# Small tiles of 32 bytes between the weight slots of an attention and feed-forward kernel

## The chip, the cores and the metric

One core of a Trainium2 chip. The metric is the device time of one execution in microseconds; lower is better. The kernel before takes 937.57 us (median of 3 runs, 937.54 to 937.85).

## The reference

Linear attention with random features, then two feed-forward layers, in float32:

```
attention, for each head:  phi(x) = exp(h - max h) / sqrt(m),  h = x omega' - |x|^2 / 2
    kv = phi(k)' v;  z = sum of phi(k);  out = phi(q) kv / (phi(q) z + 1e-6)
x = attention, 2304 tokens x 512
layer 1:  h = x @ w_in;   g = max(0.01 h, h);            x = g @ w_out      (w_in 512 x 2048, w_out 2048 x 512)
layer 2:  h = x @ w_in2;  g = h * clip(h + 3, 0, 6) / 6;  x = g @ w_out2
```

## The kernel before

The 2304 tokens go in five groups of 512, 256, 512, 512 and 512. Layer 1 takes a group at a time, and the attention of the next group lies between its matmuls; then layer 2 goes over the groups again. Every large product is made of float32 values that are split into a high and a low half of type fp32r, three matmuls for one (`mm3`, L440): high weights by high data (L441), low by high (L442), high by low (L443).

The lines name a matmul as `bank<-moving,stationary`: the operand that streams through and the weights that are loaded ahead of it. The weight loads are rows of PEld. So `bank<-x,w` is a matmul whose weights lie in a `w` slot while an `x` tile streams. The stationary operand is 128 x 128; the columns of a matmul are those of the moving one, 512 or 256.

A layer works on the 2048 hidden columns in 16 blocks of 128. In layer 1 the H part of a block moves the four `x` tiles (the split input) against a slot of `w_in`, 12 matmuls, and the O part moves the block's `g` against a slot of `w_out` into four accumulators, 12 matmuls. In layer 2 the four groups of 512 tokens take blocks in pairs (`Hpair`): the H product of two blocks is made of seven products of 256 columns (L811), whose weights are sums and differences of weight blocks, held in `w` slots (`c`), and whose moving operands are the input tiles or sums of them (`x` slots, or `w` slots). The O part moves `w_out` (512 columns of a slot) against `g` or a second `g` that lies in a `w` slot. The group of 256 tokens goes block by block with 256 columns.

All these operands live in slots, fixed tiles of SBUF that are handed out by a planner (`Graph.run`): it puts the operations of all engines in one order, by estimated costs and due times, and each operation is then emitted in that order. Its costs are of an operation's size and engine; an address is in none of them. The slots, by where they lie:
- In the pool `const`, in this order: 18 slots `w0` to `w17`, four `x`, three `g` (each two tiles of [128, 512], the halves, 2048 bytes a partition and tile), then `ident`, `wn`, `three` and `zero` (512, 512, 64 and 768 bytes).
- Behind `const`, in pools that are opened when earlier ones close: `first` (staging and attention tiles), then `second` (11 slots more of the kind `w`, L396) and `stage`, then `third` (3 more, L404). They are named `second_w` and `third_w` in the profile. Slots with an index of 24 or more are preferred for the operands of L811.
- In the pool `misc`, at the other end: staging for weights (`wst`, `wt`) and input (`xr`), scratch `u`, and small tiles: six `nm` and three pairs `den` ([128, 4, 1], 16 bytes of data in 32), three `sq`.

A tile of an operand is 2048 bytes, a multiple of 256. So all `w`, `x` and `g` tiles lie at one residue modulo 256 bytes, and `second_w` and `third_w`, behind 1856 bytes of further tiles, 64 bytes above it.

`nm` holds the negated maxima of the features (written by VectorE and POOL, read by ACT as a bias), `den` the denominators of the attention.

Of the kernel before, what the change touches and what calls it, by code (L numbers as in the profile page):

```python
# [9 lines left out]
F32R = mybir.dt.float32r  # L10
# [15 lines left out]
FT = DFF // 128  # L26
# [5 lines left out]
NLATE = 14  # L32
# [284 lines left out]
def attn_moe_kernel(ctx: ExitStack, tc: tile.TileContext, qT, kT, qn, kn, v1, om2, w1i, w1o, w2i, w2o, out):  # L317
# [6 lines left out]
    g = Graph()  # L324
# [6 lines left out]
    misc = ctx.enter_context(tc.tile_pool(name="misc", bufs=1, side="right"))  # L331
# [3 lines left out]
    def sb(name, shape, dt=F32, pool=const):  # L335
        return pool.tile(shape, dt, name=name)

    def many(n, name, *specs, pool=const):
        return [tuple(sb(f"{name}{i}_{j}", *s, pool=pool) for j, s in enumerate(specs)) for i in range(n)]

    x1 = [[dram.tile([128, 2, GN[i]], F32, name=f"x1_{i}_{k}") for k in range(KT // 2)] for i in range(NG)]

    stage = [("wst", ([128, 512, 2], U32)), ("wt", ([128, 512], U32))]
    slots = {
        "w": many(2 * FT - NLATE, "w", ([128, 512], F32R), ([128, 512], F32R)),
        "x": many(KT, "x", ([128, 512], F32R), ([128, 512], F32R)),
        "g": many(3, "g", ([128, 512], F32R), ([128, 512], F32R)),
        "wst": many(2, *stage[0], pool=misc),
        "wt": many(2, *stage[1], pool=misc),
        "xr": many(KT, "xr", ([128, 512],), pool=misc),  # L350
        "u": many(2, "u", ([128, 512],), pool=misc),
        "nm": many(6, "nm", ([128, 4, 1],), pool=misc),
        "den": many(3, "den", ([128, 4, 1],), ([128, 4, 1],), pool=misc),
        "sq": many(3, "sq", ([128, 9, 1],), pool=misc),
        "junk": many(1, "junk", ([128, 4, 128], BF16), pool=misc),
        "raw": [],
    }


    late = {  # L360
# [607 lines left out]
    for at, grp in enumerate(ORDER2):  # L968
        n = GN[grp]
# [99 lines left out]
```

## Time and profile before

| | |
|---|---|
| device time, median of 3 runs | 937.57 us |
| span of the profiled execution | 935.4 us |
| TensorE matmul busy | 926.9 us (99%) |
| TensorE weight load busy (beside matmuls) | 785.2 us (84%) |
| VectorE busy | 595.2 us (64%) |
| ScalarE busy | 521.0 us (56%) |
| GpSimd busy | 239.6 us (26%) |
| share of TensorE in the chain that ended last | 95% |
| granted TensorE clock, all 40 slices | 0.9 or more |

A matmul's duration in the profile is longer than the distance to the next matmul's start, since matmuls overlap; the busy time is the union. A mean of a group mixes the first matmul of a block, which may wait for its operand, with the others.

### The profile page before, as it was taken

What the parts mean: (1) busy time and instruction counts of PE and PEld (TensorE: products, weight loads), DVE (VectorE), ACT (ScalarE), POOL (GpSimd) and SP (SyncE); (2) the same over time, 40 slices, a digit from 0 to 9 for tenths busy, and PEclk for the clock granted to TensorE, in tenths of its full rate; (3) what the DMA queues carried; (4) which work ended last, traced back from release to release, by engine and by line L of the source; (5) the groups of instructions that cost most, each with busy time, mean ns of one, the idle gap of its engine ahead of it and who ended that gap; (6) DMA issues with size and microseconds to landing.
All of it is one profiled execution on the core that took longest, in us unless ns stands there. A gap on an engine that the chain in (4) does not pass through costs nothing.

```text
span 935.4 us, 15350 instructions
## 1 busy us (share of the span) xinstructions
PE 926.9 (99%) x5678; PEld 785.2 (84%) x5678; DVE 595.2 (64%) x1373; ACT 521.0 (56%) x1207; POOL 239.6 (26%) x349
## 2 busy tenths in 40 slices
PE   8999999999999999999999999999999999999998
PEld 8878777899778787777788898888888888888887
DVE  6898978734732223233587799888669657865642
ACT  7867767754643344333433576567566556655543
POOL 3445444312410012111000023343334234330000
PEclk9999999999999999999999999999999999999999
DMA  9457645333211211000454341101002000200010
GB/s 330 137 163 233 186 141 157 110 90 87 63 40 40 67 45 57 12 0 1 158 158 135 113 159 55 59 22 69 1 1 69 23 1 1 68 1 1 2 46 22
DMA packets 40186, 73.04 MB, mean 78 GB/s; under 512 B 10032, under 2 KB 19376, under 8 KB 40112
## 3 DMA queue, kind: packets, MB, share of 16 engines
q1 hardware_dynamic: 40112, 72.07, 24.2%
q8 instruction: 44, 0.72, 0.3%
q14 instruction: 30, 0.25, 0.1%
HBM read 62.62 MB, written 9.44 MB: 77 GB/s over the span
## 4 chain that ended last, share of the span: by engine, by line
PE 95%; DVE 2%; ACT 1%; DMA 0%; issue 0%; SPq 0%; POOL 0%
PE bank L441 23%; PE bank L442 22%; PE bank L443 22%; PE bank L811 16%; PE bank L563 4%; PE bank L609 3%; PE bank L739 2%; PE bank L716 1%; PE bank L620 1%; PE bank L650 1%; ACT first_h L543 1%; DMA first_xn<-kn 0%; DVE second_w L430 0%; PE bank L584 0%; DVE wst L474 0%
## 5 line engine op out<-in xcount | busy, mean ns | idle before, releaser
L874 DVE TENSOR_TENSOR g<-bank,g 128x512 fp32r<-128x512 f32 (+1 forms) x96 | 57.6, 600 | 120.8 <-ACT g L427 120.5
L872 ACT ACTIVATE bank<-bank 128x512 f32<-128x512 f32 (+1 forms) x80 | 43.8, 547 | 103.8 <-PE bank L443 103.6
L532 DVE TENSOR_REDUCE nm<-bank 128x4 f32<-128x512 f32 (+3 forms) x92 | 49.5, 568 | 53.5 <-PE bank L563 53.0
L427 ACT COPY late_u<-bank 128x256 f32<-128x256 f32 (+1 forms) x103 | 38.9, 380 | 79.3 <-PE bank L811 75.3
L543 ACT ACTIVATE h<-bank,nm 128x128 f32<-128x128 f32 x208 | 58.6, 391 | 29.6 <-POOL nm L538 29.3
L538 POOL TENSOR_TENSOR nm<-nm,sq 128x4 f32<-128x4 f32 (+3 forms) x92 | 21.9, 251 | 196.3 <-DVE nm L535 194.3
L441 PE MATMUL bank<-x,w 128*128 128x512 f32 (+1 forms) x188 | 70.8, 377 | 0.0
L441 PE MATMUL bank<-g,w 128*128 128x512 f32 (+1 forms) x180 | 69.2, 384 | 0.0
L443 PE MATMUL bank<-x,w 128*128 128x512 f32 (+1 forms) x188 | 68.7, 366 | 0.0
L442 PE MATMUL bank<-x,w 128*128 128x512 f32 (+1 forms) x188 | 68.6, 365 | 0.0
L443 PE MATMUL bank<-g,w 128*128 128x512 f32 (+1 forms) x180 | 66.4, 369 | 0.0
L442 PE MATMUL bank<-g,w 128*128 128x512 f32 (+1 forms) x180 | 66.3, 368 | 0.0
L441 PE MATMUL bank<-x,second_w 128*128 128x512 f32 (+1 forms) x160 | 57.2, 357 | 0.0
L442 PE MATMUL bank<-x,second_w 128*128 128x512 f32 (+1 forms) x160 | 55.8, 349 | 0.0
L443 PE MATMUL bank<-x,second_w 128*128 128x512 f32 (+1 forms) x160 | 55.8, 349 | 0.0
L442 PE MATMUL bank<-w,g 128*128 128x512 f32 x138 | 54.5, 395 | 0.0
L427 ACT CAST g<-bank 128x512 fp32r<-128x512 f32 (+1 forms) x95 | 49.5, 521 | 8.8 <-DVE bank L869 6.5
L441 PE MATMUL bank<-w,g 128*128 128x512 f32 x138 | 54.3, 394 | 0.0
L443 PE MATMUL bank<-w,g 128*128 128x512 f32 x138 | 53.8, 390 | 0.0
L811 PEld LDWEIGHTS bank<-x,second_w 128*128 128x128 f32 x330 | 42.2, 188 | 3.6 <-ACT late_u L427 2.0
L811 PE MATMUL bank<-x,second_w 128*128 128x256 f32 x330 | 44.8, 281 | 0.0
L441 PEld LDWEIGHTS bank<-x,w 128*128 128x128 f32 x188 | 35.4, 188 | 9.8 <-issue 3.0
(274 smaller groups left out, 2597.0 us busy)
## 6 DMA issues: line engine op xcount, KB each, us to landing
wst<-w2i SPq DMA_DIRECT2D x16, 512.0 KB, 3.5
wst<-w2o SPq DMA_DIRECT2D x16, 512.0 KB, 3.6
v<-v SPq DMA_DIRECT2D x14, 330.0 KB, 3.0
wst<-w1i SPq DMA_DIRECT2D x9, 512.0 KB, 4.3
wst<-w1o SPq DMA_DIRECT2D x9, 512.0 KB, 4.2
xr<-x SPq DMA_DIRECT2D x16, 256.0 KB, 3.3
xn<-kn SPq DMA_DIRECT2D x14, 256.0 KB, 2.9
xT<-kT SPq DMA_DIRECT2D x13, 256.0 KB, 2.7
```

The costliest lines, as they stand in the source:

```text
L427: return [("act", c_act(n, psum), lambda: nc.scalar.copy(dst(), src())), dve if psum else dve + (True,)]
L441: nc.tensor.matmul(o, lhsT=ah, rhs=bh, start=start, stop=False)
L442: nc.tensor.matmul(o, lhsT=al, rhs=bh, start=False, stop=False)
L443: nc.tensor.matmul(o, lhsT=ah, rhs=bl, start=False, stop=stop)
L532: g.op([("dve", c_dve(c * 128), lambda raw=raw, n_=n_: nc.vector.tensor_reduce(out=n_()[:, :, 0], in_=raw(), axis=AX.X, op=ALU.min))], rd= ...
L538: ("pool", 170, lambda n_=n_, s_=s_: nc.gpsimd.tensor_tensor(out=n_(), in0=n_(), in1=s_(), op=ALU.subtract))],
L543: nc.scalar.activation(h.tiles[0][:, q * 128:q * 128 + 128], raw()[:, q], AF.Exp, bias=nm.tiles[0][:, q], scale=-1.0)
L563: nc.tensor.matmul(ps[bank].tiles[0][o, i * 128:i * 128 + 128], lhsT=src.tiles[0][r, i * 128:i * 128 + n], rhs=wn[r], start=True, stop=True)
L609: nc.tensor.matmul(p.tiles[0][:, w], lhsT=l, rhs=r, start=n == 0, stop=n == len(todo) - 1, skip_group_check=True)
L811: nc.tensor.matmul(R[r](), lhsT=w[x], rhs=m[y], start=start and k == i == 0, stop=k == 1 and i == 2, skip_group_check=True)
L872: g.op([("act", c_act(n, True), lambda: nc.scalar.activation(P(), P(), AF.Prelu, alpha=0.01))], wr=[p], due=d)
L874: g.op([("dve", c_dve(n), lambda: nc.vector.tensor_tensor(out=G1(), in0=P(), in1=G0().bitcast(F32), op=ALU.subtract))], rd=[p, (gg, 0)], w ...
```

## The change

Ten of the small tiles (six `nm`, four `den`) move from `misc` to `const`: one behind every second `w` slot up to the sixteenth, one behind `g0` and one behind `g1`. The last pair of `den` stays in `misc`, behind `sq`, which moves ahead of `wst`. Each takes 32 bytes a partition. The number of slots of each kind stays, and so does the sum of bytes in use. By the sizes, relative to `x`: `w0`, `w1` at residue 0, `w2`, `w3` at 32, and so on to `w14`, `w15` at 224 and `w16`, `w17` at 0; `g0`, `g1`, `g2` at 0, 32 and 64; `second_w` and `third_w` at 128.

```diff
--- before.py
+++ after.py
@@ -341,20 +341,37 @@
     x1 = [[dram.tile([128, 2, GN[i]], F32, name=f"x1_{i}_{k}") for k in range(KT // 2)] for i in range(NG)]
 
     stage = [("wst", ([128, 512, 2], U32)), ("wt", ([128, 512], U32))]
+    small = {"nm": [], "den": []}
+    shifts = ["nm"] * 6 + ["den"] * 5
+
+    def shift():
+        t = shifts.pop(0)
+        small[t].append(sb(f"{t}{len(small[t])}", [128, 4, 1]))
+
+    def spread(n, name, every):
+        out = []
+        for i in range(n):
+            out.append(tuple(sb(f"{name}{i}_{j}", [128, 512], F32R) for j in range(2)))
+            if i % every == every - 1 and i < n - 1:
+                shift()
+        return out
+
     slots = {
-        "w": many(2 * FT - NLATE, "w", ([128, 512], F32R), ([128, 512], F32R)),
+        "w": spread(2 * FT - NLATE, "w", 2),
         "x": many(KT, "x", ([128, 512], F32R), ([128, 512], F32R)),
-        "g": many(3, "g", ([128, 512], F32R), ([128, 512], F32R)),
+        "g": spread(3, "g", 1),
+        "sq": many(3, "sq", ([128, 9, 1],), pool=misc),
         "wst": many(2, *stage[0], pool=misc),
         "wt": many(2, *stage[1], pool=misc),
         "xr": many(KT, "xr", ([128, 512],), pool=misc),
         "u": many(2, "u", ([128, 512],), pool=misc),
-        "nm": many(6, "nm", ([128, 4, 1],), pool=misc),
-        "den": many(3, "den", ([128, 4, 1],), ([128, 4, 1],), pool=misc),
-        "sq": many(3, "sq", ([128, 9, 1],), pool=misc),
         "junk": many(1, "junk", ([128, 4, 128], BF16), pool=misc),
         "raw": [],
     }
+    while len(small["den"]) < 6:
+        small["den"].append(sb(f"den{len(small['den'])}", [128, 4, 1], pool=misc))
+    slots["nm"] = [(x,) for x in small["nm"]]
+    slots["den"] = list(zip(small["den"][::2], small["den"][1::2]))
 
 
     late = {
```

## Rows read from the trace of the kernel before

**Rows 1.** The page, parts 1 and 4: busy us (share, instructions); share of the chain.

```profile
PE 926.9 (99%) x5678; PEld 785.2 (84%) x5678; DVE 595.2 (64%) x1373; ACT 521.0 (56%) x1207; POOL 239.6 (26%) x349
...
PE 95%; DVE 2%; ACT 1%; DMA 0%; issue 0%; SPq 0%; POOL 0%
```

**Rows 2.** Waits of the weight loads: us in total, times, longest.

```profile
PEld bank L811 <- ACT late_u L427: 6.1, 30, 0.3
```

**Rows 3.** L441 from 461 to 504: ns min/median/max, first and last start.

```profile
L441 PE MATMUL bank<-x,w x35: 389/389/389, 460.8 to 503.0; 128*128 128x512 f32 x35
L441 PE MATMUL bank<-g,w x29: 389/389/389, 465.6 to 503.7; 128*128 128x512 f32 x29
```

**Rows 4.** The same line from 511 to 545, two groups of four.

```profile
L441 PE MATMUL bank<-x,second_w x20: 393/396/398, 511.9 to 536.4; 128*128 128x512 f32 x20
...
L441 PE MATMUL bank<-g,third_w x4: 393/396/398, 542.7 to 544.8; 128*128 128x512 f32 x4
```

**Rows 5.** Stretches: length, PE, PEld, DVE, ACT, POOL busy us, clock, DMA share, GB/s.

```profile
460.00:500.00 40.00, 40.00 (x178) 33.12 (x177) 29.31 (x52) 16.56 (x28) 2.19 (x2) 1.00 0.45 143
511.00:545.00 34.00, 34.00 (x147) 27.42 (x146) 28.14 (x51) 16.28 (x31) 2.93 (x2) 1.00 0.29 91
```

**Rows 6.** Groups by form, layer 1, 512 columns: busy us, mean ns | idle before.

```profile
L442 PE MATMUL bank<-x,w 128*128 128x512 f32 x144 | 56.2, 390 | 0.0
...
L442 PE MATMUL bank<-x,second_w 128*128 128x512 f32 x96 | 37.9, 395 | 0.0
...
L442 PE MATMUL bank<-g,second_w 128*128 128x512 f32 x80 | 31.6, 396 | 0.0
...
L442 PE MATMUL bank<-g,third_w 128*128 128x512 f32 x32 | 12.7, 396 | 0.0
```

**Rows 7.** Groups by form, layer 2, 512 columns.

```profile
L442 PE MATMUL bank<-w,g 128*128 128x512 f32 x138 | 54.5, 395 | 0.0
...
L443 PE MATMUL bank<-w,g 128*128 128x512 f32 x138 | 53.8, 390 | 0.0
...
L442 PE MATMUL bank<-w,w 128*128 128x512 f32 x56 | 21.9, 391 | 0.0
...
L442 PE MATMUL bank<-w,second_w 128*128 128x512 f32 x40 | 15.8, 395 | 0.0
...
L443 PE MATMUL bank<-second_w,w 128*128 128x512 f32 x20 | 7.9, 394 | 0.0
L442 PE MATMUL bank<-second_w,w 128*128 128x512 f32 x20 | 7.8, 391 | 0.0
```

**Rows 8.** L442 from 217.4 to 221, 256 columns: ns min/median/max.

```profile
L442 PE MATMUL bank<-x,second_w x7: 276/276/279, 217.6 to 221.0; 128*128 128x256 f32 x7
```

**Rows 9.** Groups by form, 256 columns.

```profile
L811 PE MATMUL bank<-x,second_w 128*128 128x256 f32 x330 | 44.8, 281 | 0.0
...
L811 PE MATMUL bank<-x,third_w 128*128 128x256 f32 x258 | 34.9, 281 | 0.0
L811 PE MATMUL bank<-second_w,second_w 128*128 128x256 f32 x234 | 32.8, 282 | 0.0
...
L811 PE MATMUL bank<-x,w 128*128 128x256 f32 x180 | 25.9, 284 | 0.0
...
L442 PE MATMUL bank<-x,second_w 128*128 128x256 f32 x64 | 17.9, 279 | 0.0
...
L811 PE MATMUL bank<-second_w,w 128*128 128x256 f32 x54 | 7.5, 280 | 0.0
```

**Rows 10.** ACT's groups by line: busy us, mean ns | idle before, releaser.

```profile
L427 ACT CAST second_w<-wst 128x512 fp32r<-128x512 f32 x33 | 20.5, 622 | 3.8 <-DVE wst L434 3.1 <-PE bank L811 0.3
...
L427 ACT CAST w<-wt 128x512 fp32r<-128x512 f32 x16 | 10.0, 624 | 13.7 <-DVE wt L483 13.7
```

**Rows 11.** Timeline of TensorE, second and eighth matmul after a break: start us, us.

```profile
86.64 0.39 PE L442 MATMUL bank<-g,w 128*128 128x512 f32 x1
...
88.03 0.39 PE L442 MATMUL bank<-g,w 128*128 128x512 f32 x1
```

## The prediction

> **What bounds the kernel now.** I read the page's busy table and the chain first: TensorE is busy 926.9 of 935.4 us and holds 95% of the chain [rows 1]. So a step of another engine counts only where TensorE waits for it, and its largest wait of that kind, 6.1 us in 30 pieces, is for values copied out of PSUM [rows 2]. The span is 2.2 us below the 937.57 us median; I take that remainder as constant and add changes to the median.
>
> What is left is how long TensorE needs for one matmul. Two views say that this is not one number. From 460.8 to 503.7 us every first matmul of a triple takes 389 ns [rows 3]: 64 of them, 63 steps of three matmuls in 42.9 us, 227.0 ns apart. From 511.9 to 544.8 us the same shape takes 393 to 398 ns [rows 4] (two of four such groups stand there): 48 of them, 47 steps, 32.9 us / 141 = 233.3 ns apart. So duration and spacing differ alike (6.5 and 6.3 ns), and durations stand for spacings below. Both stretches have full clock and a TensorE that never pauses; VectorE is busy 73% in one and 83% in the other, DMA 45% and 29% [rows 5], no likely cause of 6.5 ns on every matmul. What differs without exception is the stationary operand, `w` slots in one, `second_w` and `third_w` in the other. By the sizes of their tiles `w`, `x` and `g` lie at one residue modulo 256 and the later slots 64 bytes above it. The groups of all lines agree [rows 6]: 390 against 395 or 396.
>
> So I read a price per pair of residues: (residue of the weights) minus (residue of the moving tile). At 512 columns: offset 0 costs 1 ns above 389 on average, +64 costs 6.5 [rows 6], −64 (`second_w` moving against `w`) 2 to 5 [rows 7]. At 256 columns it is the other way round: the shortest row is 276 ns at +64 [rows 8], in most of layer 2 the same offset shows 281, offset 0 shows 282 to 284, −64 shows 280 [rows 9].
>
> **The change part by part.** Order, waits, DMAs and counts stay as they are: the planner's costs hold no address. ACT's casts take 622 ns into `second_w` and 624 into `w` [rows 10], two residues 64 apart, so I cost the new residues at nothing for ACT, and likewise for VectorE and POOL, which write the low halves and the small tiles that move; the cover, if that is wrong, is that TensorE waits little for any of them [rows 2]; without it, 2 ns on the some 1200 instructions of ACT [rows 1] would be 2.4 us. What remains is TensorE's price list. After the change the 18 `w` slots lie at eight residues (four of them at that of `x`, two at each other), `g` at 0, +32 and +64, and `second_w` and `third_w` at +128 from `x`, because ten small tiles push the pools behind them by 320 bytes. Five of the eight offsets (32, 96, 128, 160, 224) occur nowhere in the trace. The nearest rows are +1 and +6.5 at 512 columns, with −64 at 2, 2 and 5 in between; I take 2.5 for an offset that is not 0 or +64, with 1 and 6.5 as ends. At 256 columns the ends are 0 and 8 and the nearest rows (−64, 280; +64, 281) give 4; for +128 I take 3.5, for the rest 4.
>
> Layer 1, 512 columns, weights in `w`: 144 a line with `x` moving and as many with `g`, on three lines, 864 matmuls [rows 6], now +1. After: 4/18 at 1, 2/18 at 6.5, 12/18 at 2.5, mean 2.6. That is +1.4 us (ends +0.5 and +3.7).
> Layer 1, weights in later slots: 3 x (96 + 16 + 80 + 32) = 672 [rows 6] (the 16 are `x` against `third_w`, like the 32 with `g`), now +6.5. Moving `x` (336) goes to 128, 2.5: −1.3. Moving `g` (336) goes to 128, 96 and 64, mean (2.5 + 2.5 + 6.5) / 3 = 3.8: −0.9. Sum −2.2 (ends −3.1 and 0).
> Layer 2, 512 columns, `w` or `second_w` moving: 828 matmuls, among them `w` against `g` 414 at about +4, `w` against `second_w` 120 at +6, `w` against `w` 168 at +2.3 [rows 7], 3.3 us of excess in all. After: spread over eight offsets, (1 + 6.5 + 6 x 2.5) / 8 = 2.8 each, 2.3 us: −1.0 (ends −1.9 and +1.5).
> 256 columns, `x` against later slots: 828 matmuls, 330 + 258 in L811 and 48 at +5, 192 at +3 [rows 9]: 3.8 us. After, at 3.5: 2.9, so −0.9 (ends −3.8 and +2.9). `x` against `w`, 180 in L811 [rows 9] and 132 in L441 to L443, at +7.5: spread 4/18 at 7.5, 14/18 at about 4, mean 4.8: −0.8 (ends −1.7 and 0). `g` against `w`, 108, in the same ratio: −0.2. The 414 products with both operands in later slots, 234 of them `second_w` with itself [rows 9], keep their offset 0, since both move together: 0, and 0 for the 162 mixed ones, which have no common direction.
> Settling: in a run at offset 0 that follows a break, the six steps from its second matmul on take 1.39 us, 231.7 ns each where 227.0 is the settled value [rows 11], 28 ns for six. Today neighbouring blocks of 12 matmuls have one offset; with alternating slot residues each of 128 layer-1 blocks may settle anew, at most 3.6 us. Part of it is already in the mean prices, so +1.5 (ends 0 and 3.6).
>
> Sum: 1.4 − 2.2 − 1.0 − 0.9 − 0.8 − 0.2 + 1.5 = −2.2 us, 935.4 us; I give **935.5 us**, the rounding of the terms being of that size. All ends together would be 927 and 949.
>
> The rule that speaks against any effect: the Trainium skill, "TensorE: Matmul & The Clock Gate", section "Step-by-step: what each phase is for", says that the running matmul and the loading of the next weights read SBUF through two separate ports, so that one takes nothing from the other; "SBUF — State Buffer", section "Who interferes with whom", says that TensorE never waits on anyone. By these the sum would be zero. The rows do not bear that out: one shape, one clock, 227.0 and 233.3 ns [rows 3, 4].
>
> **The rivals.**
> F, faster: only the offsets +64 at 512 columns and 0 at 256 are bad, and every other one is about as good as the best. With 1.5 for the untried ones at 512 columns and 3 at 256, the parts are +0.8, −2.8, −1.6, −2.5 and 0.5 for settling: −5.6, **932.0 us**. For it: at 256 columns the best offset is +64, so 0 is nothing special. Against: −64 already costs 2 to 5 at 512.
> S, slower: the low price at offset 0 is a lock that any other offset loses. Place: the 864 layer-1 matmuls on `w`, of which 14/18 leave offset 0. With 5.5 for the untried ones at 512 and 5 at 256 the parts are +3.1, −0.6, +0.9, −0.2 and +1.5: +4.7, **942.3 us**. The point from which it decides: with p the price of the untried offsets at 512, the three 512-column terms sum to 1.76 p − 6.2 us; with −1.8 and +1.5 added, the total passes +1.9 us at p = 4.8 and falls below −1.9 at p = 2.6. For it: 64 of 64 durations at 389 look like a lock, and +64 loses it fully. Against: −64 loses only a third to a half of it.
> N, nothing: the difference belongs to the slot itself or to its time in the kernel, not to the residues. Then **937.6 us**. For it: `second_w` and `third_w` are used late, with other neighbours on the engines. Against: within layer 2 `w` and `second_w` alternate and keep their own prices [rows 7].
> A part of N can also hold: the change gives `second_w` and `third_w` one residue, not eight, so more than half of the 256-column matmuls see one new offset or none.
>
> **How the numbers follow.** About 0.2% (1.9 us) is what a measurement tells from no change, so "same" is 935.7 to 939.4. The forecast (p between 1.8 and 4.8, own range 934 to 939) has 0.47: it lies across the border, 0.20 of it faster, 0.27 same. F has 0.20, all faster. S has 0.23, all slower. N has 0.07, same. The rest, 0.03, is half faster, half slower. Faster 0.42, same 0.34, slower 0.24. The range reaches into F and S until about 0.1 is left beyond each end: 931.0 to 942.2.
>
> **What would show it.** In the changed kernel's groups by form, `x` against `w` at 512 columns no longer has one duration of 389 ns over a whole stretch but steps from block to block with the slot (389 at four slots of 18); its mean of 390 rises to some 391 or 392 (S: 394 and more; F: under 390.5; N: unchanged). `x` against `second_w` at 512 columns falls from 395 to about 391.5 (S: 394; F: 390). In L811 `x` against `second_w` goes from 281 to between 276 and 284, and `second_w` against `second_w` stays at 282. Neither VectorE's nor ACT's durations move, and the waits [rows 2] stay within a microsecond. The forecast is wrong if 389 and 396 appear as before with the same slots, if the +128 price at 256 columns is at 0 or 8 (3 us either way), or if TensorE's idle time grows, which nothing in this sum holds.

## The result and the profile after

The changed kernel takes 943.7 us (942.79 to 943.8), 1.0061 times the kernel before (interval 1.0042 to 1.0081): 6.1 us slower. The span of the profiled execution is 942.0 us, where 935.4 us stood before. Line numbers are 17 higher than before: L458 to L460 are the three lines of `mm3`, L828 is L811.

The page of the changed kernel, parts 1 and 4:

```profile
PE 933.9 (99%) x5678; PEld 788.0 (84%) x5678; DVE 594.8 (63%) x1373; ACT 521.5 (55%) x1207; POOL 240.4 (26%) x349
...
PE 95%; DVE 2%; ACT 1%; DMA 0%; issue 0%; SPq 0%; POOL 0%
```

TensorE's busy time grew by 7.0 us, from [rows 1], with the same 5,678 matmuls; VectorE, ScalarE and GpSimd stand within a microsecond, and the chain has the same shares. So TensorE doesn't wait more for the other engines: the matmuls themselves became slower.

The groups of the changed kernel by form (busy us, mean ns | idle before), first 512 columns, then 256:

```profile
L459 PE MATMUL bank<-g,w 128*128 128x512 f32 x144 | 56.6, 393 | 0.0
L459 PE MATMUL bank<-x,w 128*128 128x512 f32 x144 | 56.7, 394 | 0.0
L459 PE MATMUL bank<-x,second_w 128*128 128x512 f32 x96 | 37.8, 394 | 0.0
L459 PE MATMUL bank<-g,second_w 128*128 128x512 f32 x80 | 31.6, 395 | 0.0
...
L459 PE MATMUL bank<-w,g 128*128 128x512 f32 x138 | 54.5, 395 | 0.0
L460 PE MATMUL bank<-w,g 128*128 128x512 f32 x138 | 54.5, 395 | 0.0
L459 PE MATMUL bank<-w,w 128*128 128x512 f32 x56 | 22.1, 394 | 0.0
...
L828 PE MATMUL bank<-x,second_w 128*128 128x256 f32 x330 | 45.5, 283 | 0.0
L828 PE MATMUL bank<-x,w 128*128 128x256 f32 x180 | 25.8, 283 | 0.0
L828 PE MATMUL bank<-second_w,second_w 128*128 128x256 f32 x234 | 32.7, 282 | 0.0
```

`x` against `w`, 390 ns in [rows 6], takes 394, and `g` against `w` takes 393; its row in the kernel before:

```profile
L442 PE MATMUL bank<-g,w 128*128 128x512 f32 x144 | 56.1, 390 | 0.0
```

The later slots, which were to gain from offset 128, stay at 394 and 395. In layer 2 `w` against `g` has lost the 390 of one of its lines [rows 7] and `w` against `w` goes from 391 to 394. At 256 columns `x` against `second_w` rises from 281 to 283 [rows 9], and `second_w` against itself, whose two operands move together, keeps 282.

The first line of a triple between 461 and 504 us, the stretch of [rows 3], as min/median/max:

```profile
L458 PE MATMUL bank<-x,w x32: 389/394/404, 462.8 to 501.2; 128*128 128x512 f32 x32
L458 PE MATMUL bank<-g,w x28: 391/396/401, 468.3 to 504.0; 128*128 128x512 f32 x28
```

Before, each of these was 389. In this stretch `x` meets eight slots, one at each residue, and `g` none at its own. The `x` blocks at the offsets 0 and 32, four matmuls of this line each:

```profile
L458 PE MATMUL bank<-x,w x4: 389/389/393, 462.8 to 464.8; 128*128 128x512 f32 x4
L458 PE MATMUL bank<-x,w x4: 392/395/396, 465.5 to 467.6; 128*128 128x512 f32 x4
```

Only the block at the residue of `x` keeps 389. The step from block to block with the slot, which the prediction named as its sign, is there; its height is that of rival S.

The remaining steps of the prediction: the waits of the weight loads (us in total, times, longest), then ACT's casts into `w` (busy us, mean ns | idle before), then the first stretch of [rows 5] with the same columns:

```profile
PEld bank L828 <- ACT late_u L444: 5.8, 28, 0.3
```

```profile
L444 ACT CAST w<-wt 128x512 fp32r<-128x512 f32 x16 | 10.0, 623 | 13.1 <-DVE wt L500 13.1
```

```profile
460.00:500.00 40.00, 40.00 (x174) 32.31 (x173) 26.65 (x47) 16.88 (x28) 1.29 (x1) 1.00 0.45 144
```

Against [rows 2] and [rows 10] next to nothing moved: 5.8 for 6.1 us, 623 for 624 ns. The clock is 1.00 again and TensorE never stops, but 40 us hold 174 matmuls where they held 178.

### The profile page after: what moved, and what is told of

The parts are those of the page before. It is cut to its first block, busy times and chain, and to the rows that moved or that the text cites. A ratio compares the mean times of both kernels' runs of the same rounds, so it can differ in the third digit from the quotient of the medians.

```text
span 942.0 us, 15350 instructions
## 1 busy us (share of the span) xinstructions
PE 933.9 (99%) x5678; PEld 788.0 (84%) x5678; DVE 594.8 (63%) x1373; ACT 521.5 (55%) x1207; POOL 240.4 (26%) x349
## 4 chain that ended last, share of the span: by engine, by line
PE 95%; DVE 2%; ACT 1%; DMA 0%; issue 0%; SPq 0%; POOL 0%
PE bank L458 23%; PE bank L460 22%; PE bank L459 22%; PE bank L828 16%; PE bank L580 4%; PE bank L626 3%; PE bank L756 2%; PE bank L733 1%; PE bank L637 1%; PE bank L667 1%; ACT first_h L560 1%; DMA xn<-qn 0%; DVE second_w L447 0%; PE bank L601 0%; DVE wst L491 0%
## 5 line engine op out<-in xcount | busy, mean ns | idle before, releaser
L458 PE MATMUL bank<-x,w 128*128 128x512 f32 (+1 forms) x188 | 71.2, 379 | 0.0
L458 PE MATMUL bank<-g,w 128*128 128x512 f32 (+1 forms) x180 | 69.7, 387 | 0.0
L460 PE MATMUL bank<-x,w 128*128 128x512 f32 (+1 forms) x188 | 69.1, 368 | 0.0
L460 PE MATMUL bank<-g,w 128*128 128x512 f32 (+1 forms) x180 | 66.8, 371 | 0.0
L458 PE MATMUL bank<-x,second_w 128*128 128x512 f32 (+1 forms) x160 | 57.2, 358 | 0.0
L460 PE MATMUL bank<-x,second_w 128*128 128x512 f32 (+1 forms) x160 | 55.9, 349 | 0.0
L460 PE MATMUL bank<-w,g 128*128 128x512 f32 x138 | 54.5, 395 | 0.0
L458 PE MATMUL bank<-w,g 128*128 128x512 f32 x138 | 54.4, 395 | 0.0
L828 PEld LDWEIGHTS bank<-x,second_w 128*128 128x128 f32 x330 | 42.8, 188 | 3.7 <-ACT late_u L444 2.1
L828 PE MATMUL bank<-x,second_w 128*128 128x256 f32 x330 | 45.5, 283 | 0.0
L458 PEld LDWEIGHTS bank<-x,w 128*128 128x128 f32 x188 | 35.3, 188 | 10.3 <-issue 3.0
```

The source lines that it names most:

```text
L458: nc.tensor.matmul(o, lhsT=ah, rhs=bh, start=start, stop=False)
L460: nc.tensor.matmul(o, lhsT=ah, rhs=bl, start=False, stop=stop)
L828: nc.tensor.matmul(R[r](), lhsT=w[x], rhs=m[y], start=start and k == i == 0, stop=k == 1 and i == 2, skip_group_check=True)
```

## Where the 6 us lie

The start times of single matmuls give more than the durations. I took each distance to the next start less 226.7 ns (512 columns) or 113.3 ns (256 columns), left out gaps above 25 ns, which are stops and not prices, and summed by the terms of the prediction. Each pair is counted by the weights that are loaded while the tile moves, those of the next matmul, so the counts differ a little from those of the groups. The profile's names have no slot numbers; the program emits its 4,320 fp32r matmuls in the order in which the trace has them, and so each one's tiles and addresses are known.

| term | matmuls | before, us | after, us | change | predicted |
|---|---|---|---|---|---|
| layer 1, 512 columns, weights in `w` | 830 | 1.1 | 4.1 | +3.0 | +1.4 |
| layer 1, 512 columns, weights in later slots | 644 | 4.1 | 3.8 | −0.3 | −2.2 |
| layer 2, 512 columns | 863 | 3.3 | 4.8 | +1.4 | −1.0 |
| 256 columns, `x` against later slots | 810 | 2.4 | 4.3 | +1.8 | −0.9 |
| 256 columns, `x` against `w` | 293 | 1.6 | 1.4 | −0.2 | −0.8 |
| 256 columns, `g` moving | 175 | 0.6 | 0.8 | +0.2 | −0.2 |
| 256 columns, both in later slots | 377 | 2.1 | 2.1 | −0.1 | 0 |
| 256 columns, the rest | 242 | 1.0 | 1.3 | +0.3 | 0 |

The prices' changes sum to +6.1 us, and the gaps above 25 ns together change by −0.3; 0.8 of the 6.6 us by which the span grew lie outside these pairs. The places are those of the prediction; almost every size is off towards slower, at 512 columns because the untried offsets cost more than I gave them.

Which of the two weights sets the price, those in use or those being loaded, isn't shown. In long runs both lie at one offset. Where they differ the traces point both ways: in the kernel before, 72 matmuls of 512 columns with their own weights at offset 0 and the next at 64 cost 1.1 ns, where 6.7 stands with both at 64; with the later slots at 128 the same step, from 0 to 128, costs 5.2.

## The experiments

Offset theory: what a matmul costs hangs on the residue modulo 256 of the weights (counted, as above, by those loaded meanwhile) minus that of the moving tile. Rivals: the small tiles in the operands' pool; the slots themselves and their neighbours in time; the change of residue from one block to the next.

**The small tiles alone.** They move as in the change, but behind all operands of `const` (the edit is against the changed kernel), with padding that keeps every offset.

```diff
-        "w": spread(2 * FT - NLATE, "w", 2),
+        "w": many(2 * FT - NLATE, "w", ([128, 512], F32R), ([128, 512], F32R)),
...
-        "g": spread(3, "g", 1),
+        "g": many(3, "g", ([128, 512], F32R), ([128, 512], F32R)),
...
+    slots["nm"] = many(6, "nm", ([128, 4, 1],))
+    den = [sb(f"den{i}", [128, 4, 1]) for i in range(4)]
+    sb("pad", [128, 48])
...
```

> The small tiles move as in the change, but all behind the operands and padded, so that w, x and g keep one residue and second_w and third_w stay 64 bytes above it. Offset theory (the price of a matmul hangs on the residue of the weights loaded meanwhile minus that of the moving tile): no offset changes, 937.6 us within 1 us. Rival, the small tiles: that nm and den are written and read in the pool of the operands, or that the attention's pools shift by 64, costs the 6 us: 943 us.

938.06 us, ratio 1.0005 (0.9996 to 1.0014); summed prices −0.1 us. The rival that the small tiles cost the time is out.

**Only the later slots, to 128.** The kernel before, with one pad ahead of the pool of `second_w`.

```diff
         zero = sb("zero", [128, 192], F32R)
+        sb("pad", [128, 16])
```

> Only second_w and third_w move, from 64 to 128 above x; w, x and g keep one residue. Offset theory with the mean spacings of the changed kernel's trace (512 columns: offset 64 at 6.3 ns above the base, 128 at 5.7; 256 columns: 3.0 at 64, 5.4 at 128): 512 columns -0.2 us, 256 columns +2.3 us, so 939.7 us. The prediction's prices (2.5 and 3.5) gave -2.9 us, 934.7. Rival, alternation (any operand pattern that stays the same over blocks is cheap): no change, 937.6.

940.86 us, ratio 1.0033 (1.0020 to 1.0045), 3.1 us more. The groups by form of this kernel:

```profile
L811 PE MATMUL bank<-x,second_w 128*128 128x256 f32 x330 | 45.8, 284 | 0.0
L442 PE MATMUL bank<-x,second_w 128*128 128x512 f32 x96 | 37.9, 394 | 0.0
```

At 512 columns the later slots gain nearly nothing (394 for 395); at 256 columns `x` against `second_w` goes from 281 to 284, which over 810 matmuls is +2.4 us by the start times. Offset 128 is bad at both sizes. (The 3.0 at 64 in the expectation is what the kernel before shows; the 77 matmuls left at 64 in the changed kernel show 3.9.) The size came out a microsecond above the expectation: with one offset left for 1,070 matmuls, 128 costs 6.1 ns, not the 5.4 it showed among the mixed ones, and gaps add 0.7 us. The alternation rival fails, since nothing alternates here that did not before.

**Only the spread of `w` and `g`.** The change, with a pad that puts the later slots back to 64.

```diff
         zero = sb("zero", [128, 192], F32R)
+        sb("pad", [128, 48])
```

> The change with 192 bytes of padding behind g, so that second_w and third_w lie again 64 above x; the w slots at eight residues and the g at three, as in the change. Offset theory by the changed kernel's prices: 512 columns +3.4 us, 256 columns +0.1, so 941.1 us, and with e2 it adds up to about the whole change. Rival, the far slots carry the loss: 938.

941.16 us, ratio 1.0034 (1.0022 to 1.0046), 3.4 us more; layer 1 on `w` +3.1 us, layer 2 at 512 columns +1.4, as in the whole change. With the 3.1 of the kernel before it, 6.5, which is the 6.1 within the intervals. So the change is two losses, of like size when each stands alone: the spread spoils 512 columns, and the push behind it spoils 256. In the changed kernel, by the table, the 512 columns have 4.1 us of it and the 256 columns 2.0.

**The later slots at offset 0.** The same edit on the kernel before.

> The kernel before with second_w and third_w at the residue of w, x and g: every offset is 0. Offset theory: at 512 columns all 2,337 matmuls get 1.3 to 2.4 ns in place of 6.3 for 829 of them (-3.4 to -5 us), at 256 columns 1,070 go from 3.0 to 5.5 (+2.5 us): between 935.0 and 936.7. Rival, the slot (late slots cost more wherever they lie): x against second_w stays at 395 ns, 937.6 us or above.

936.82 us, ratio 0.9990 (0.9981 to 0.9999). The groups by form of this kernel:

```profile
L442 PE MATMUL bank<-x,second_w 128*128 128x512 f32 x96 | 37.4, 390 | 0.0
L811 PE MATMUL bank<-x,second_w 128*128 128x256 f32 x330 | 45.7, 284 | 0.0
```

The late slots take 390 at 512 columns once they lie at the residue of `x`: it was never the slot or its time in the kernel. Layer 1 on later slots gives back 3.4 us and layer 2 0.7, and 256 columns take 2.4 (`x`) and 1.2 (the others) of it away (284, the price of offset 0). This is the trade inside one layout: 512 columns want 0, 256 columns do not.

**One constant new offset.** A pad of 32 bytes between `w` and `x`, so that all of layer 1 on `w` has offset 224 in long runs.

```diff
+    w = many(2 * FT - NLATE, "w", ([128, 512], F32R), ([128, 512], F32R))
+    sb("pad", [128, 8])
     slots = {
-        "w": many(2 * FT - NLATE, "w", ([128, 512], F32R), ([128, 512], F32R)),
+        "w": w,
```

> One pad of 32 bytes between w and x: all w keep one residue, x and g lie 32 above it, second_w and third_w stay 64 above x. So every layer-1 matmul on w has one and the same new offset (224, that is -32) in long runs, without any alternation between blocks. Offset theory, by the spacings of the changed kernel's trace (224 at 6.3 ns at 512 columns, 3.9 at 256): 942.1 us (512 columns +4.9, 256 columns -0.3), x against w at 512 columns 394 or more. Rival, alternation: what costs is the change of residue from block to block, a constant one settles: 937.6, x against w at 390.

942.76 us, ratio 1.0051 (1.0037 to 1.0064). The groups by form of this kernel:

```profile
L444 PE MATMUL bank<-x,w 128*128 128x512 f32 x144 | 56.9, 395 | 0.0
L444 PE MATMUL bank<-x,second_w 128*128 128x512 f32 x96 | 37.9, 395 | 0.0
```

`x` against `w` now stands where only the later slots stood before. One pad of 32 bytes costs 4.8 us, with nothing alternating. The loss is the offset itself, not its change from block to block.

**All operands moved together.** 64 bytes of padding ahead of everything.

```diff
+    sb("pad", [128, 16])
     slots = {
```

> 64 bytes of padding ahead of everything in the pool: every operand moves by 64, all offsets between weights and moving tiles stay. Offset theory: 937.6 us within 1 us, and the groups by form keep their means. Rival, the absolute residue: the 512-column groups change by up to 6 ns, 2 to 8 us.

938.15 us, ratio 1.0001 (0.9992 to 1.0010). The absolute residue is without effect; the difference decides.

**The price by itself.** 768 matmuls behind the end, 48 for each offset and size, with the layout of the next kernel.

```diff
         g.run(slots, len(banks) - 1, phase, [phase2, phase3, phase4])
+        wb = slots["w"][0][0]
+        for n in (512, 256):
+            for o in range(8):
+                at = 8 * (8 - o) if o else 0
+                for i in range(48):
+                    nc.tensor.matmul(banks[0][0][:, :n], lhsT=wb[:, i % 4 * 128:i % 4 * 128 + 128], rhs=xall[:, 16 + at + 512:16 + at + 512 + n],
+                                     start=True, stop=True)
```

> The kernel of e7 with a tail of 768 further matmuls on operands already in place, whose results are not used: 48 for each of the eight offsets in steps of 32 bytes, at 512 and at 256 columns, weights in one w slot. It measures the disputed price alone, at one offset for a long run. Offset theory: settled spacings above the base of some 0 to 1 (offset 0) and 6 to 7 ns (32, 64, 96, 160, 224), some 3 (192) and 5 to 6 (128) at 512 columns; at 256 columns near 0 at 64 and 5 to 7 at 0, 96, 128 and 160. Rival, slots and neighbours: all eight alike, since nothing else runs.

This kernel was executed once, and the runs of the tail are compared within that execution. One line of the tail, in a window inside each run: ns min/median/max, first and last start. First 512 columns at the offsets 0, 32, 64, 96, 128, 160, 192, 224, then 256 columns at 0, 64, 128 and 192:

```profile
L1018 PE MATMUL bank<-xall,w x39: 389/389/389, 930.6 to 939.2; 128*128 128x512 f32 x39
L1018 PE MATMUL bank<-xall,w x39: 395/396/396, 941.5 to 950.4; 128*128 128x512 f32 x39
L1018 PE MATMUL bank<-xall,w x39: 393/393/398, 952.7 to 961.6; 128*128 128x512 f32 x39
L1018 PE MATMUL bank<-xall,w x39: 392/397/400, 963.9 to 972.8; 128*128 128x512 f32 x39
L1018 PE MATMUL bank<-xall,w x40: 390/393/404, 974.9 to 984.0; 128*128 128x512 f32 x40
L1018 PE MATMUL bank<-xall,w x39: 392/394/399, 986.3 to 995.2; 128*128 128x512 f32 x39
L1018 PE MATMUL bank<-xall,w x39: 388/392/394, 997.5 to 1006.2; 128*128 128x512 f32 x39
L1018 PE MATMUL bank<-xall,w x39: 393/396/397, 1008.5 to 1017.4; 128*128 128x512 f32 x39
...
L1018 PE MATMUL bank<-xall,w x31: 283/283/283, 1019.7 to 1023.3; 128*128 128x256 f32 x31
L1018 PE MATMUL bank<-xall,w x30: 281/281/281, 1031.1 to 1034.5; 128*128 128x256 f32 x30
L1018 PE MATMUL bank<-xall,w x31: 279/281/285, 1042.4 to 1046.0; 128*128 128x256 f32 x31
L1018 PE MATMUL bank<-xall,w x30: 276/276/276, 1053.9 to 1057.2; 128*128 128x256 f32 x30
```

With 512 columns only offset 0 has one duration of 389, at 192 it is close (median 392), and six offsets lie at medians of 393 to 397. By the starts of the last 40 matmuls of each run:

| offset | 0 | 32 | 64 | 96 | 128 | 160 | 192 | 224 |
|---|---|---|---|---|---|---|---|---|
| 512 columns, ns apart | 226.7 | 233.3 | 233.4 | 234.4 | 232.5 | 233.3 | 228.9 | 233.3 |
| 256 columns, ns apart | 120.0 | 118.2 | 117.8 | 118.6 | 118.8 | 120.1 | 113.3 | 116.7 |

At 512 columns the expectation holds within 1 ns in every column. At 256 it fails in one place: 64 is not near 0 but at 117.8, and the shortest spacing is at 192. In the kernel before, 113.3 ns (276) stood at 64 [rows 8]. So at 256 columns ±64 has two levels, and the offset alone does not say which.

**A layout for both sizes.** The later slots at 0, and `x` as one large tile that layer 1 reads at the residue of `w` and layer 2 64 bytes below, where only the tail of its neighbour lies that layer 1 no longer needs. A mark `far` on a buffer, set for layer 2's `x`, chooses the view.

```diff
...
+    sb("pad0", [128, 48])
+    xall = sb("xall", [128, 16 + 2 * KT * 512], F32R)
+    xview = lambda o: [tuple(xall[:, o + (2 * i + h) * 512:o + (2 * i + h + 1) * 512] for h in range(2)) for i in range(KT)]
+    Graph.FAR = xview(0)
...
-        "x": many(KT, "x", ([128, 512], F32R), ([128, 512], F32R)),
+        "x": xview(16),
...
-                b.tiles = slots[b.tag][b.slot]
+                b.tiles = self.FAR[b.slot] if b.far else slots[b.tag][b.slot]
...
         zero = sb("zero", [128, 192], F32R)
+        sb("pad", [128, 48])
```

> second_w and third_w at the residue of w, and x as one large tile that layer 1 reads at the residue of w and layer 2 64 bytes below, so that x against any weights is 0 at 512 columns and +64 at 256. Order and counts as before. Offset theory: 512 columns as in the kernel with the far slots at 0 (-4.3 us), 256 columns 960 matmuls at 64 (2.5 ns) and 937 at 0 (6 ns), 8.0 in place of 7.6 us: 933.7 us, with 933 to 935 as the range. Rival, the gain at 512 columns cannot be had together with +64 at 256 (the writers of x are slowed, or the waits change): 936.5 or above.

934.77 us, ratio 0.9966 (0.9954 to 0.9978), 3.2 us below the kernel before and 8.9 us below the changed one. The groups by form of this kernel:

```profile
L448 PE MATMUL bank<-xall,second_w 128*128 128x512 f32 x96 | 37.4, 390 | 0.0
L822 PE MATMUL bank<-xall,second_w 128*128 128x256 f32 x330 | 45.1, 282 | 0.0
```

The 512 columns keep all of their gain (390, −3.4 us in layer 1 on later slots, −0.9 in layer 2); at 256 columns 64 costs 4.1 ns here, not the 2.5 expected, the 117.8 of the tail almost throughout. The rival (936.5 or above) is out. The run also bears on the modulus: `x` in layer 1 now lies an odd multiple of 256 bytes from `w`, where it lay a multiple of 512 before, and its matmuls against `w` cost 1.3 ns for 1.4. With offset 128 costing 5.7 at 512 columns, the step that fits is 256 bytes.

**Layer 2's `x` above the weights.** The views exchanged, so that layer 2 has offset 192 (the tiles stand in reverse order in the large one, so that again only a neighbour that is done with is overwritten, and the pads follow).

```diff
-    Graph.FAR = xview(0)
+    Graph.FAR = xview(16)
...
-        "x": xview(16),
+        "x": xview(0),
```

> As e7, but layer 2 reads x 64 bytes above the weights' residue in place of 64 below, offset 192 in place of 64 for the 960 matmuls of 256 columns with x moving; 512 columns as in e7. Offset theory by the tail of e8 (256 columns: 113.3 ns at 192, 117.8 at 64): if those settled spacings hold between other matmuls, 960 go from 4.1 to near 0.5 above the base, -3.4 us from e7, 931.4 us; if the breaks and the matmuls at offset 0 around them keep them at the 5.1 that 103 matmuls at 192 show in the kernel before, +1 us, 935.8. Rival, the tail's price is one of its own regular pattern of weights: at or above e7, 934.8.

936.02 us, ratio 0.9981 (0.9972 to 0.9990). A group by form of this kernel:

```profile
L822 PE MATMUL bank<-xall,second_w 128*128 128x256 f32 x330 | 45.2, 281 | 0.0
```

The 960 matmuls at 192 cost 4.6 ns each, near the 5.1 that stood in the kernel before, not the 0 of the tail. The means of the durations hide this: 281 ns here, 282 in the kernel with 64, which is the faster one. The tail's 113.3 does not carry over to layer 2, whose products are six matmuls long and pass between high and low tiles; whether that is the reason wasn't tried. What chooses between the two levels at 256 columns is open.

## Why the prediction was wrong, point by point

*The bound was right.* TensorE's own spacing carries the time: other engines' times and TensorE's waits stayed, and its busy time rose by 7.0 us where the span rose by 6.6.

*The reading of the rows was right.* Price by offset of weights to moving tile, 0 best at 512 columns, +64 costing 6.5: shown by the later slots at offset 0 (390 for 395), by the constant 32 bytes (395 for 390), and by moving everything (no change). Rival N, by which the placement does nothing, falls. The rule of the Trainium skill ("TensorE: Matmul & The Clock Gate", section "Step-by-step: what each phase is for") says that loading the next weights takes nothing from the running matmul. The sum of zero that I drew from it does not agree with these runs: one pad of 32 bytes between weights and moving tiles costs 4.8 us. Where in the reading of the two operands the price arises is not shown.

*The step that failed is the price p of the untried offsets at 512 columns.* I took 2.5 ns, leaning on −64 "at 2, 2 and 5 in between" the ends of 1 and 6.5. That row was the exception. Five untried offsets cost 5.8 to 7.7 in the tail (232.5 to 234.4 less 226.7), which is the row of +64; only −64 is at 2.2. In the sum of 512-column terms, 1.76 p − 6.2, p = 6 in place of 2.5 gives +4.4 for the +4.1 measured. My own point of decision stood at p = 4.8. The trace held two offsets other than 0, one at 2 to 5 and one at 6.5, and I leaned on the cheaper, although rival S had the argument for the dearer: 64 of 64 equal durations at offset 0 look like a lock, which other offsets lose.

*Three prices at 256 columns were mis-sized too.* For +128 I took 3.5, and it measured 5.4 in the changed kernel, 6.1 with only the later slots moved and 5.5 in the tail (118.8 ns less 113.3). For the offsets of the kernel before I took mean durations, 4.5 ns at +64 (3.8 us for 828 matmuls) and 7.5 at 0, where the start times give 3.1 and 5.3: those means hold the first matmuls of a block, which wait, and that durations stand for spacings had been tested at 512 columns alone. The first two errors, of like size, turned −0.9 into +1.8 us for `x` against later slots. The best level at 64 was known from [rows 8], and I should have asked what leaving it costs: most of the distance to offset 0, as at 512 columns.

*Settling* was +1.5 and came to little: the spacings in the mixed kernel (6.2 to 7.0 ns at the untried offsets, 128 at 5.7) are within 1 ns of those of the tail's long runs. Only offset 0 shows it, 2.4 to 3.0 for `x` and `g` in the changed kernel in place of some 1.3, and there are 175 such matmuls left: 0.2 to 0.3 us.

*The other engines:* nothing for ACT (623 ns), nothing for the small tiles (ratio 1.0005), as costed.

*What came about is rival S*, place and price: 5.5 for the untried offsets at 512 columns and 5 at 256 gave 942.3 us; the run gave 943.7. Its +3.1 for layer 1 on `w` is the +3.0 measured. That its total comes so close is in part luck: it had −0.2 at 256 columns, where +2.0 was measured, and +1.5 for settling, which hardly came. Nor does every other offset lose the low price: at −64 the tail shows 2.2 ns, at the other six 5.8 to 7.7. Its sign for `x` against `w` at 512 columns (394 and more) is in the rows above. The range ended at 942.2, just under its centre, because S had been given 0.23; with its argument weighed evenly the range would have had to reach past it.

## What to carry to other kernels

For fp32r matmuls of 512 columns, place the operands that meet on TensorE at one residue modulo 256 bytes, and look at the difference between the weights and the moving tile: spreading addresses is no way to avoid a conflict when the aligned case is the cheap one (226.7 ns against 232.5 to 234.4 at six of the seven others). At 256 columns the aligned case is dear (120.0), so in a kernel with both sizes the gain is a trade: all operands at one residue gave 0.9 us, with a place of its own for the `x` of layer 2 it became 3.2. When durations of one shape fall into two values by operand name in a trace, compare the operands' addresses before the neighbours in time. A mean duration is not a spacing where it holds matmuls that wait: take prices from start times. And price an untried point by the reason behind the known ones, not by the cheapest neighbour.

## What was not expected of the hardware

A pad of 32 bytes that no instruction reads costs 4.8 us of 937.9 (0.5%), since it moves 1,177 matmuls of 512 columns to an offset of 32 or 224 and 245 to 96 or 160. Matmuls of 512 columns at offset 0 go 226.7 ns apart with one duration, at −64 228.9, at six other offsets 232.5 to 234.4. At 256 columns offset 0 is near the worst (120.0), and at ±64 there are two levels, 113.3 and 117.8 ns, whose choice these runs don't explain.
